# Softmax division moved from the weights to the weighted sum in ten head pairs of a fused mixer

## The chip, the cores and the metric

One Trainium2 chip, one of its cores. The metric is the device time of one execution in microseconds (us). The kernel before took 956.19 us (median of 3 runs, 954.49 to 959.67). Engines are named as in the profile: PE (TensorE, its weight loads PEld), DVE (VectorE), ACT (ScalarE), POOL (GpSimd) and SP, which issues the DMAs.

## The reference

Attention over 4 batches of 12 heads (448 tokens, head size 64), then two mixers (weights `moe_*` and `moe2_*`) on its output of 4 x 448 x 768. All in float32. What the change touches is the attention:

```python
q_n, k_n = (rmsnorm(q, g_q), rmsnorm(k, g_k))
scores = scale * np.matmul(q_n, k_n.transpose(0, 1, 3, 2))
scores = scores - np.max(scores, axis=-1, keepdims=True)
attn = np.exp(scores)
attn = attn / (np.sum(attn, axis=-1, keepdims=True) + 1e-09)
return np.matmul(attn, v).astype(np.float32)
```

The first mixer is relu, a split into two halves, a normalisation, a product over the tokens, a gate and an output product. The second mixes tokens (448 to 256 to 448), then channels (768 to 1536 to 768).

## The kernel before

The 48 heads run as 24 pairs of two heads (`NP`, line 809), six pairs (`KD`) to a batch. A pair goes through these steps, each on four chunks (`C`) of 112 query rows (`T`):

- `norms` and `scale` (lines 622 to 639): row norms of q and k, and the product with them, the latter one POOL operation of 112x1024 in place on `raw`.
- `transposed` (641): q and k turned by PE into a PSUM tile `tp`, copied out by ACT. For the first eight pairs (`WHOLE`) as one float32 tile `whole`, later as a high and a low part.
- `scores` (667): PE writes the scores of both heads to two `sc` tiles; DVE takes the negated maximum `nm`; ACT writes `e`, the exponential, and its row sums to `sums`.
- `normalise` (694): DVE adds 1e-9 to the sums and takes the reciprocal, then POOL multiplies each 112x448 block of `e` in place, eight blocks to a pair.
- `turned` (705): PE transposes `e` (28 transposes to a pair, four to a `tp` tile); ACT or, for two of seven, DVE copies `tp` to `et`.
- `values` (722): PE multiplies by v into the PSUM tile `av`; ACT copies `av` to the high part of `xp`, DVE subtracts to its low part, POOL copies the last tokens to `xr`.

`slot(s)` (773) lists the steps of one slot: the early steps of pair s, and `normalise` of its second half, `turned` and `values` of pair s-1. Beside them the program lists the preparation of weights (`prepare_v`, `prepare_uo`, `prepare_next`: `word`, `wpart`, `wv`) and the first mixer of a batch (`moe`: `vps`, `ups`, `sps`, `xps`), which needs all six pairs of that batch. Then follow the tokens and the channels of the second mixer (`u_ps`, `h1ps`, `h2ps`, `o_ps`).

None of that is the order on the chip. Every operation goes to `Plan`, which knows a cost and a delay for each (`estimate`, line 214) and what it depends on. `issue` (364) places all operations eight times with these costs (`place`), always by due times found from the end backwards, and emits the order of the shortest planned span. So one changed cost can move any operation of the program. A DMA costs max(475, bytes/260) ns there and is taken to land 2000 ns later (line 244). PSUM banks, eight in all, are given out by the plan as well.

Of the kernel before, what the change touches and what calls it, by code (L numbers as in the profile page):

```python
# [12 lines left out]
F32 = mybir.dt.float32  # L13
F32R = mybir.dt.float32r
U32 = mybir.dt.uint32
AF = mybir.ActivationFunctionType
ALU = mybir.AluOpType
# [4 lines left out]
HI, LO = 0, 1  # L22
# [127 lines left out]
class Plan:  # L150
# [63 lines left out]
    def estimate(self, engine, fn, out, ins, kwargs):  # L214

        shape = max((tuple(x.shape) for x in [out] + ins if isinstance(x, Part)), key=free)
        n = free(shape)
        psum = any(x.tile.psum for x in ins)
        if engine == "tensor":
            if fn == "transpose":  # L220
                return ins[0].shape[0] / 1.2 + 3, 200
            n = free(ins[1].shape)
            if ins[1].dtype == F32R:
                return 0.326 * n if ins[0].shape[0] <= 64 else n / 2.4 + 13, 200
            if ins[0].shape[0] <= 64:
                return 1.04 * n, 200
            return n / 1.2 + 54 if out.shape[0] <= 64 else n / 0.6, 200
        if engine == "scalar":
            extra = any(isinstance(kwargs.get(k), Part) for k in ("bias", "scale"))
            extra += kwargs.get("accum_out") is not None  # L230
            return 0.833 * n + (51 if psum else 94) + 93 * extra, 142
        if engine == "vector":
            if n <= 64:
                return 160, 128
            if fn in ("tensor_scalar", "tensor_copy") and not psum:
                return 0.53 * n + 90, 128
            pointer = fn == "scalar_tensor_tensor" and any(free(x.shape) == 1 for x in ins)
            return 1.042 * n + 70 + 61 * pointer, 175 if free(out.shape) < n else 128
        if engine == "gpsimd":
            if fn == "tensor_scalar":  # L240
                return max(165, 1.3 * n + 35), 75
            pace = 2.0 if any(x.steps and x.steps[-1][0] == "to_broadcast" for x in ins) else 2.4
            return max(165, pace * n + 20), 75
        return max(475, shape[0] * n * 4 / 260), 2000

    def fence(self, pools, act):

# [173 lines left out]
def free(shape):  # L421
    n = 1
    for x in shape[1:]:
        n *= x
    return n
# [11 lines left out]
def attention_moe_mixer(  # L437
# [7 lines left out]
    nc = tc.nc  # L445
    B, H, S, D = q.shape
# [5 lines left out]
    P = 128  # L452
    C = 4
    T = S // C
# [83 lines left out]
    ident = const.tile([P, P], F32)  # L538
    make_identity(nc, ident)
    nc = Plan(nc)  # L540

    def opened(stack, name, **kind):
        return stack.enter_context(tc.tile_pool(name=name, bufs=2, **kind))
# [15 lines left out]
    psum = Banks(opened(ctx, "psum", space=PSUM))  # L559

    def mm_tile(name):
        return psum.tile([P, 512], "mm", name)
# [20 lines left out]
    class Attention:  # L583
# [3 lines left out]
        def __init__(self, stack):  # L587
            self.p = Pool(opened(stack, "attn", side="right"))
            self.raw, self.v32, self.r = {}, {}, {}
            self.qt, self.kt, self.e, self.et, self.av = {}, {}, {}, {}, {}  # L590
            self.sums = {}

        def load(self, i):
            if not 0 <= i < NP:
# [46 lines left out]
        def transposed(self, i, a):  # L641
# [6 lines left out]
            tpf = tp.rearrange("p c t -> p (c t)")  # L648
            if i < WHOLE:
                to = self.qt if a == 0 else self.kt  # L650
# [16 lines left out]
        def scores(self, i, c):  # L667
            if not 0 <= i < NP:
                return
            p = self.p  # L670
            if c % 2 == 0:
                self.sums[i, c] = p.tile([P, 4], F32, tag="sum", bufs=4, name="sums")
            sums, qt, kt = self.sums[i, c - c % 2], self.qt[i], self.kt[i]
            nm = p.tile([P, 2], F32, tag="nm", bufs=4, name="nm")
            e = p.tile([T, 2, S], F32, tag="e", bufs=6, name="e")
            sc = [psum.tile([P, 512], "sc", "sc")[:T, :S] for _ in range(2)]
            cs = slice(c * T, (c + 1) * T)
            with nc.joined_up():
                for n, (x, w) in enumerate(PASSES[:1] if i < WHOLE else PASSES):
                    for r in range(2):  # L680
                        me = slice(r * D, (r + 1) * D)
                        if i < WHOLE:
                            nc.tensor.matmul(sc[r], qt[me, cs], kt[me], start=True, stop=True)
                        else:
                            nc.tensor.matmul(
                                sc[r], qt[me, x, cs], kt[me, w], start=n == 0, stop=n == len(PASSES) - 1)
            for r in range(2):
                nc.vector.reduce_max(nm[:T, r:r + 1], sc[r], axis=AX.X, negate=True)
                at = c % 2 * 2 + r
                nc.scalar.activation(  # L690
                    e[:, r], sc[r], AF.Exp, bias=nm[:T, r:r + 1], scale=1.0, accum_out=sums[:T, at:at + 1])
            self.e[i, c] = e

        def normalise(self, i, c0):
            if not 0 <= i < NP:
                return
            sums = self.sums[i, c0][:T]
            nc.vector.tensor_scalar(sums, sums, 1e-9, None, ALU.add)
            nc.vector.reciprocal(sums, sums)
            for c in range(c0, c0 + 2):  # L700
                for r in range(2):
                    e, at = self.e[i, c][:, r], c % 2 * 2 + r
                    nc.gpsimd.tensor_scalar(e, e, sums[:, at:at + 1], 1.0, ALU.mult, ALU.mult)

        def turned(self, i, n):

            if not 0 <= i < NP:
                return
            r, kc = n % 2, n // 2
            t = kc * P + r * (S + R)  # L710
            tp = psum.tile([P, C, T], "tp", "tp")
            for c in range(C):
                nc.tensor.transpose(
                    tp[:, c, :], self.e[i, c].rearrange("p r k -> p (r k)")[:, t:t + P], ident[:T, :T])
            et = self.et[i, n] = self.p.tile([P, S], F32, tag="et", bufs=7, name="et")
            tpf = tp.rearrange("p c t -> p (c t)")
            if n in ON_DVE:
                nc.vector.tensor_copy(et, tpf)
            else:
                nc.scalar.activation(et, tpf, AF.Copy)  # L720

        def values(self, i, kc):

            if not 0 <= i < NP:
                return
            b, j = divmod(i, KD)
            if kc == 0:
                self.av[i] = mm_tile("av")
            av = self.av[i]
            v32, rest = self.v32[i]  # L730
            with nc.joined_up():
                for r in range(2):
                    lhs = v32[:, r, kc] if kc < C - 1 else rest[:, r]
                    rhs = self.et[i, 2 * kc + r if kc < C - 1 else 2 * kc]
                    nc.tensor.matmul(
                        av[r * D:(r + 1) * D, :S], lhs, rhs, start=kc == 0, stop=kc == C - 1)
            if kc < C - 1:
                return

            at = i % XB  # L740
            on = pairs if any(n % XB == at for n in range((B - 1) * KD, NP)) else self.p
            x = on.tile([P, 2, S], F32R, tag=f"xp{at}", bufs=1, name="xp")
            nc.scalar.activation(x[:, HI], av[:, :S], AF.Copy)
            nc.vector.tensor_tensor(x[:, LO], av[:, :S], x[:, HI].bitcast(F32), op=ALU.subtract)
            xr = on.tile([P, 2, R], F32R, tag=f"xr{at}", bufs=1, name="xr")
            nc.gpsimd.tensor_copy(xr, x[:, :, LAST:].bitcast(F32))
            xs_of.setdefault(b, []).append(x)
            xr_of.setdefault(b, []).append(xr)
            self.v32.pop(i)
# [58 lines left out]

    NP = NH // 2
    VB, XB = 2, 9  # L810
    WHOLE = 8
    ON_DVE = (3, 5)
    SLOT = 10
    PREP0, LAG, SPAN = 1, 0.5, 6
# [405 lines left out]
    n = NP + 1  # L1220
# [4 lines left out]
    at = Attention(early)  # L1225
# [79 lines left out]
```

## Time and profile before

| what | us |
|---|---|
| median of 3 runs | 956.19 |
| the profiled execution's own time | 952.84 |
| span of that execution, first to last instruction | 951.1 |
| PE busy in it | 915.1 |
| DVE busy | 567.9 |
| ACT busy | 452.1 |
| POOL busy | 370.1 |

The span is 1.7 us shorter than the execution's own time, which lies 3.4 us under the median. Busy time is the union of the intervals in which an engine had an instruction; since the ends of matmuls are modelled and they overlap in the pipeline, a busy PE need not be at its peak. The granted clock is TensorE's, as a share of 2.4 GHz; its lower level is 1.2 GHz.

### The profile page before, as it was taken

To read this page: it belongs to the slowest core of one execution; us is meant where nothing else is said; L and a number is where in the kernel's file an instruction comes from. 1 tells how busy PE (TensorE), PEld (TensorE's weight loads), DVE (VectorE), ACT (ScalarE), POOL (GpSimd) and SP (SyncE) were. 2 spreads that over 40 slices of the span, in tenths; PEclk is the share of its full clock that TensorE was granted. 3 is DMA by queue.
4 is the path that set the end of the run, shared out by engine and by line. 5 is a ranking of instruction groups with operands and counts; after the bars stand their busy time and mean duration, and the time that the engine had idled before them with its cause. 6 is when DMAs were issued, how large, how long until landed. Compare 5 with 4: busy or idle time off the path is not lost.

```text
span 951.1 us, 15484 instructions
## 1 busy us (share of the span) xinstructions
PE 915.1 (96%) x5328; PEld 736.9 (77%) x5328; DVE 567.9 (60%) x1254; ACT 452.1 (48%) x1135; POOL 370.1 (39%) x538
## 2 busy tenths in 40 slices
PE   3898999999999999999999999999999999999998
PEld 1344366668767777677889999899898998999898
DVE  4787878775776767764151367534665556555434
ACT  5887877777676777765342345301312213122100
POOL 3767766785666664654124123101201102011100
PEclk9998999999999999999999999999999999999999
DMA  6544465666534565332673475721211212111024
GB/s 153 138 101 134 116 172 149 158 188 184 163 92 107 172 207 179 97 98 99 220 223 129 142 246 181 266 85 34 78 56 36 64 34 83 50 51 50 17 89 144
DMA packets 124654, 118.58 MB, mean 125 GB/s; under 512 B 74784, under 2 KB 108128, under 8 KB 123040
## 3 DMA queue, kind: packets, MB, share of 16 engines
q1 hardware_dynamic: 124576, 117.59, 41.0%
q8 instruction: 42, 0.69, 0.3%
q14 instruction: 36, 0.29, 0.1%
HBM read 89.77 MB, written 27.79 MB: 124 GB/s over the span
## 4 chain that ended last, share of the span: by engine, by line
PE 82%; ACT 5%; DVE 5%; DMA 3%; issue 2%; POOL 2%; SPq 1%; ACTq 0%; POOLq 0%; DVEq 0%
PE o_ps L405 18%; PE h2ps L405 18%; PE tp L405 9%; PE av L405 6%; PE xps L405 6%; PE ups L405 6%; PE sc L405 6%; PE sps L405 4%; PE u_ps L405 3%; PE h1ps L405 3%; PE vps L405 3%; ACT e L405 2%; DVE nm L405 1%; SPq L405 1%; DMA x<-x_d 1%
## 5 line engine op out<-in xcount | busy, mean ns | idle before, releaser
L405 PE MATMUL o_ps<-c,h 128*128 128x384 f32 x1008 | 179.7, 337 | 0.0
L405 PE MATMUL h2ps<-ut,c 128*128 128x512 f32 (+1 forms) x864 | 178.9, 364 | 0.0
L405 PEld LDWEIGHTS o_ps<-c,h 128*128 128x128 f32 x1008 | 175.0, 188 | 2.0 <-DVE acc L405 0.5
L405 PEld LDWEIGHTS h2ps<-ut,c 128*128 128x128 f32 x864 | 148.1, 189 | 24.3
L405 POOL TENSOR_SCALAR e<-e,sums 112x448 f32<-112x448 f32 x192 | 122.8, 656 | 63.0 <-DVE sums L405 35.1
L405 POOL TENSOR_TENSOR c<-word,c 128x384 fp32r<-128x384 f32 x40 | 40.5, 1014 | 265.1 <-ACT c L405 241.7
L405 ACT ACTIVATE e<-sc,nm 112x448 f32<-112x448 f32 x192 | 120.0, 637 | 29.1 <-PE tp L405 15.0
L405 DVE TENSOR_REDUCE nm<-sc 112x1 f32<-112x448 f32 x192 | 110.0, 614 | 22.3 <-PE sc L405 22.0
L405 PEld LDWEIGHTS tp<-ident,e 112*128 112x128 f32 x672 | 75.3, 142 | 47.0 <-POOL e L405 16.6
L405 PE MATMUL tp<-ident,e 112*128 112x112 f32 x672 | 101.9, 267 | 6.4 <-POOL e L405 3.2
L405 DVE TENSOR_TENSOR acc<-o_ps,acc 128x384 f32<-128x384 f32 x140 | 77.2, 555 | 29.6 <-PE o_ps L405 28.9
L405 ACT ACTIVATE h<-h2ps 128x512 fp32r<-128x512 f32 (+1 forms) x48 | 25.8, 538 | 116.5 <-PE h2ps L405 114.9
L405 ACT ACTIVATE c<-word 128x384 fp32r<-128x384 f32 x40 | 21.0, 525 | 123.0 <-DVE word L405 58.2
L405 DVE SCALAR_TENSOR_TENSOR h<-h2ps,h 128x512 fp32r<-128x512 f32 (+1 forms) x48 | 29.9, 624 | 82.3 <-ACT h L405 82.2
L405 ACT ACTIVATE et<-tp 128x448 f32<-128x448 f32 x120 | 63.4, 544 | 20.5 <-PE tp L405 19.9
L405 PE MATMUL ups<-xp,wu 128*128 128x448 f32 x288 | 69.6, 379 | 1.4 <-ACT vr L405 0.7
L405 PE MATMUL av<-et,v 128*64 128x448 f32 x288 | 67.4, 563 | 0.0
L405 PE MATMUL xps<-wo,g 128*128 128x256 f32 x432 | 63.3, 291 | 0.1
L405 PEld LDWEIGHTS xps<-wo,g 128*128 128x128 f32 x432 | 55.1, 190 | 5.0 <-issue 2.3
L405 PEld LDWEIGHTS ups<-xp,wu 128*128 128x128 f32 x288 | 51.7, 189 | 8.6 <-ACT vr L405 1.1
L405 DVE TENSOR_SCALAR word<-word 128x384 f32<-128x384 f32 (+1 forms) x92 | 34.2, 372 | 37.1 <-ACT word L405 35.7
L405 PE MATMUL vps<-wv,xp 128*128 128x512 f32 x216 | 55.1, 402 | 0.0
(105 smaller groups left out, 1414.5 us busy)
## 6 DMA issues: line engine op xcount, KB each, us to landing
raw<-in_moe_w_ch_dram SPq DMA_DIRECT2D x40, 384.0 KB, 3.2
wu<-wu_d SPq DMA_DIRECT2D x16, 768.0 KB, 5.1
wo<-wo_d SPq DMA_DIRECT2D x12, 1024.0 KB, 5.1
raw<-in_q_dram SPq DMA_DIRECT2D x48, 112.0 KB, 3.0
acc<-u_d SPq DMA_DIRECT2D x14, 384.0 KB, 8.2
out_dram<-o SPq DMA_DIRECT2D x28, 192.0 KB, 1.9
v<-in_v_dram SPq DMA_DIRECT2D x48, 96.0 KB, 2.6
x_d<-xo SPq DMA_DIRECT2D x36, 128.0 KB, 2.4
```

The costliest lines, as they stand in the source:

```text
L405: getattr(getattr(self.nc, op.engine), fn)(*args, **kwargs)
```

## The change

For the first ten pairs (`AFTER = 10`) `e` is no longer divided by its sums. `divisors` takes the reciprocals of all eight sums columns of the pair at once on DVE, has POOL spread each of them over 64 columns (`wide`), PE turn that with four transposes into a `tp` tile and ACT copy it to `over`, in which each column of `av` finds its divisor. At the end of `values`, DVE multiplies `av` by `over`, ACT copies the product to the high part of `xp` and POOL, not DVE, subtracts to the low part. The other fourteen pairs go on as before. The sums of a pair lie in one tile of eight columns, not in two of four; in the program both maxima are listed ahead of both exponentials; the ring of `et` has six places, not seven. The planned delay of a DMA is now 2400 ns and 1.2 ns for each 1000 bytes, not 2000 ns.

```diff
-        return max(475, shape[0] * n * 4 / 260), 2000
+        size = shape[0] * n * 4
+        return max(475, size / 260), 2400 + 1.2e-3 * size
...
-            if c % 2 == 0:
-                self.sums[i, c] = p.tile([P, 4], F32, tag="sum", bufs=4, name="sums")
+            if c == 0:
+                self.sums[i] = p.tile([P, 2 * C], F32, tag="sum", bufs=3, name="sums")
...
         def normalise(self, i, c0):
...
+            if i < AFTER:
+                if c0 == 2:
+                    self.divisors(i)
+                return
+            sums = self.sums[i][:T, 2 * c0:2 * c0 + 4]
...
+        def divisors(self, i):
+            p, sums = self.p, self.sums[i][:T]
+            nc.vector.tensor_scalar(sums, sums, 1e-9, None, ALU.add)
+            nc.vector.reciprocal(sums, sums)
+            wide = p.tile([T, 2 * C, D], F32, tag="wide", bufs=1, name="wide")
+            nc.gpsimd.tensor_copy(wide, sums.unsqueeze(2).to_broadcast([T, 2 * C, D]))
+            tp = psum.tile([P, C, T], "tp", "tp")
+            for c in range(C):
+                nc.tensor.transpose(
+                    tp[:, c, :], wide[:, 2 * c:2 * c + 2].rearrange("p r d -> p (r d)"), ident[:T, :T])
+            over = self.over[i] = p.tile([P, S], F32, tag="over", bufs=1, name="over")
+            nc.scalar.activation(over, tp.rearrange("p c t -> p (c t)"), AF.Copy)
...
-            et = self.et[i, n] = self.p.tile([P, S], F32, tag="et", bufs=7, name="et")
+            et = self.et[i, n] = self.p.tile([P, S], F32, tag="et", bufs=6, name="et")
...
-            nc.scalar.activation(x[:, HI], av[:, :S], AF.Copy)
-            nc.vector.tensor_tensor(x[:, LO], av[:, :S], x[:, HI].bitcast(F32), op=ALU.subtract)
+            if i < AFTER:
+                over = self.over.pop(i)
+                nc.vector.tensor_tensor(over, av[:, :S], over, op=ALU.mult)
+                nc.scalar.activation(x[:, HI], over, AF.Copy)
+                nc.gpsimd.tensor_tensor(x[:, LO], over, x[:, HI].bitcast(F32), op=ALU.subtract)
+            else:
...
+    WHOLE, AFTER = 8, 10
```

## Rows read from the trace of the kernel before

**Rows 1.** The page: busy us, share of the span and instructions of each engine.

```profile
PE 915.1 (96%) x5328; PEld 736.9 (77%) x5328; DVE 567.9 (60%) x1254; ACT 452.1 (48%) x1135; POOL 370.1 (39%) x538
```

**Rows 2.** Busy us in four stretches: PE, PEld, DVE, ACT, POOL; granted clock; DMA.

```profile
16.00:120.00 104.00, 90.35 (x477) 41.39 (x478) 84.95 (x185) 87.48 (x239) 76.69 (x122) 0.97 0.48 126
120.00:200.00 80.00, 77.00 (x464) 51.60 (x462) 61.92 (x163) 59.94 (x166) 57.05 (x88) 1.00 0.56 157
200.00:480.00 280.00, 279.07 (x1789) 207.32 (x1788) 174.44 (x415) 184.90 (x496) 157.45 (x245) 1.00 0.52 154
480.00:951.00 471.00, 466.88 (x2598) 435.17 (x2596) 243.22 (x487) 114.35 (x226) 74.76 (x71) 1.00 0.31 101
```

**Rows 3.** The same view, stretches of 8 us.

```profile
72.00:80.00 8.00, 7.12 (x42) 4.54 (x43) 5.61 (x7) 5.22 (x13) 6.05 (x10) 0.80 0.34 90
80.00:88.00 8.00, 6.33 (x24) 1.87 (x24) 6.94 (x20) 7.77 (x23) 4.41 (x8) 0.84 0.42 122
```

**Rows 4.** Waits of PE and PEld from 16 to 120 us: total, times, longest.

```profile
PE sc L405 <- ACT e L405: 3.3, 4, 1.5
PE tp L405 <- POOL e L405: 3.2, 9, 0.7
...
PEld sc L405 <- ACT e L405: 16.1, 22, 2.2
PEld tp L405 <- POOL e L405: 14.0, 23, 1.3
```

**Rows 5.** Timeline of PE: start, duration, instructions merged, idle before and its releaser.

```profile
33.25 0.93 PE L405 MATMUL tp<-ident,e 112*128 112x112 f32 x8
...
43.55 0.31 PE L405 MATMUL tp<-ident,e 112*128 112x112 f32 x1
...
71.41 0.32 PE L405 MATMUL tp<-ident,e 112*128 112x112 f32 x1 [0.30 <-POOL e L405]
...
72.61 1.70 PE L405 MATMUL tp<-ident,e 112*128 112x112 f32 x8
```

**Rows 6.** The chain that ended last, in order of time: start, duration, what.

```profile
68.60 2.77 POOL e L405 x4
```

**Rows 7.** Groups of instructions, 16 to 120 us: busy us, mean ns, idle before.

```profile
L405 POOL TENSOR_SCALAR e<-e,sums 112x448 f32<-112x448 f32 x56 | 36.9, 675 | 7.2 <-DVE sums L405 6.1 <-PE sc L405 0.7 <-DVE wpart L405 0.3
...
L405 ACT ACTIVATE et<-tp 128x448 f32<-128x448 f32 x32 | 16.7, 544 | 1.7 <-PE tp L405 1.7
...
L405 DVE TENSOR_TENSOR xp<-av,xp 128x448 fp32r<-128x448 f32 x6 | 3.7, 612 | 0.0
...
L405 DVE TENSOR_SCALAR sums<-sums 112x4 f32<-112x4 f32 x15 | 3.1, 215 | 4.1 <-ACT e L405 4.1
...
L405 DVE RECIPROCAL sums<-sums 112x4 f32<-112x4 f32 x14 | 2.3, 167 | 0.0
```

**Rows 8.** Groups of instructions, the whole trace.

```profile
L405 POOL TENSOR_TENSOR raw<-raw,ry 112x1024 f32<-112x1024 f32 x24 | 46.1, 1921 | 1.3
...
L405 POOL TENSOR_TENSOR tg<-tg,tv 128x448 f32<-128x448 f32 x16 | 18.3, 1148 | 8.3 <-DVE tv L405 5.3 <-ACT tg L405 2.7
```

**Rows 9.** The tile wpart: ns min/median/max, first and last start; then timelines of DVE and POOL.

```profile
L405 DVE TENSOR_SCALAR wpart<-wpart x88: 231/284/3223, 48.0 to 409.5; 128x256 f32<-128x256 f32 x41, 128x256 uint32<-128x256 uint32 x41, 128x192 f32<-128x192 f32 x2, 128x192 uint32<-128x192 uint32 x2
L405 DVE SCALAR_TENSOR_TENSOR wpart<-raw,wpart x88: 345/416/2368, 61.1 to 415.9; 128x256 uint32<-128x256 uint32 x82, 128x192 uint32<-128x192 uint32 x4, 64x256 uint32<-64x256 uint32 x2
...
75.48 3.22 DVE L405 TENSOR_SCALAR wpart<-wpart 128x256 f32<-128x256 f32 x1
...
75.08 2.25 POOL L405 TENSOR_TENSOR raw<-raw,ry 112x1024 f32<-112x1024 f32 x1
77.29 1.26 POOL L405 TENSOR_TENSOR wv<-word,wv 128x512 fp32r<-128x512 f32 x1
```

**Rows 10.** DMA issues: count, KB each, median us from issue to landing.

```profile
wu<-wu_d SPq DMA_DIRECT2D x16, 768.0 KB, 5.1
...
raw<-in_q_dram SPq DMA_DIRECT2D x48, 112.0 KB, 3.0
```

More of the change, by code (lines that the diff above doesn't have):

```diff
@@ L590, in __init__ @@
             self.qt, self.kt, self.e, self.et, self.av = {}, {}, {}, {}, {}
-            self.sums = {}
+            self.sums, self.over = {}, {}
         def load(self, i):
@@ L670, in scores @@
             p = self.p
-            if c % 2 == 0:
-                self.sums[i, c] = p.tile([P, 4], F32, tag="sum", bufs=4, name="sums")
-            sums, qt, kt = self.sums[i, c - c % 2], self.qt[i], self.kt[i]
+            if c == 0:
+                self.sums[i] = p.tile([P, 2 * C], F32, tag="sum", bufs=3, name="sums")
+            sums, qt, kt = self.sums[i], self.qt[i], self.kt[i]
             nm = p.tile([P, 2], F32, tag="nm", bufs=4, name="nm")
@@ L688, in scores @@
                 nc.vector.reduce_max(nm[:T, r:r + 1], sc[r], axis=AX.X, negate=True)
-                at = c % 2 * 2 + r
+            for r in range(2):
+                at = 2 * c + r
                 nc.scalar.activation(
@@ L696, in normalise @@
                 return
-            sums = self.sums[i, c0][:T]
+            if i < AFTER:
[3 more added lines that the diff above has]
+            sums = self.sums[i][:T, 2 * c0:2 * c0 + 4]
             nc.vector.tensor_scalar(sums, sums, 1e-9, None, ALU.add)
@@ L742, in values @@
             x = on.tile([P, 2, S], F32R, tag=f"xp{at}", bufs=1, name="xp")
-            nc.scalar.activation(x[:, HI], av[:, :S], AF.Copy)
-            nc.vector.tensor_tensor(x[:, LO], av[:, :S], x[:, HI].bitcast(F32), op=ALU.subtract)
+            if i < AFTER:
[4 more added lines that the diff above has]
+            else:
+                nc.scalar.activation(x[:, HI], av[:, :S], AF.Copy)
+                nc.vector.tensor_tensor(x[:, LO], av[:, :S], x[:, HI].bitcast(F32), op=ALU.subtract)
             xr = on.tile([P, 2, R], F32R, tag=f"xr{at}", bufs=1, name="xr")
@@ L810, in attention_moe_mixer @@
     VB, XB = 2, 9
-    WHOLE = 8
+    WHOLE, AFTER = 8, 10
     ON_DVE = (3, 5)
```

## The prediction

> **What bounds the kernel now.** The page's busy line came first: PE is busy 915.1 of 951.1 us, no other engine over 60% [rows 1]. So the time is PE's work and the 36 us in which PE stands still, and the next question is where these lie. The busy time by stretches answers it [rows 2]. From 200 to 480 us PE misses 0.9 us, from 480 us to the end 4.1 us. From 16 to 120 us it misses 13.65 of 104, from 120 to 200 us 3.0 of 80; what is left, some 14 us, lies ahead of the first scores, which the change doesn't reach. The stretch from 16 to 120 us is the one to read: pairs 0 to 6 without a mixer, since the first mixer needs six finished pairs. There no engine is full: PE 90.35, ACT 87.48, DVE 84.95, POOL 76.69 of 104 [rows 2]. Such a stage is bound by hand-overs between four nearly even engines.
>
> The waits of that stretch tell who is late: PE stood for ACT's exponential 3.3 us, for POOL's multiplied `e` 3.2 us in nine waits; its weight loads waited 16.1 and 14.0 us for the same two [rows 4]. The timeline of PE shows how the second looks: eight transposes of `e` at a stretch take 0.93 us, but at two places four of them run singly, each 0.31 or 0.32 us with a gap after it; there are eight such rows, the first and the last are shown [rows 5]. At the second place the chain that ended last runs through four POOL multiplications, 2.77 us [rows 6]. Right after, eight transposes took 1.70 us, not 0.93 [rows 5]: the granted clock is 0.80 in 72 to 80 us [rows 3], so 40% of that stretch was at 1.2 GHz.
>
> **The change part by part.**
>
> **POOL's multiplications go.** 56 of them took 36.9 us from 16 to 120 us [rows 7]; ten pairs have 80, about 54 us. What this is worth is not POOL's time but what PE waited: 3.2 us of idle time [rows 4], and in the eight single transposes 0.32 - 0.93/8 = 0.2 us each, 1.6 us more [rows 5]. So -4.8 us; ends 0 (the next wait, for ACT's `e` or DVE's copy, is as late) and -14.0 (all that PEld waited). After that, what comes last for the transposes is ACT's exponential itself.
>
> **The clock.** The stretch at 1.2 GHz behind the second place costs (1 - 0.80) x 8 = 1.6 us [rows 3]; I take -1.6. The next stretch, 0.84, I leave as it is. Ends 0 and -2.9 (both).
>
> **DVE under POOL.** A `wpart` operation with a median of 0.28 us lasted 3.22 us and ended when two POOL operations, 75.08 to 78.55 us, had ended; another, 0.42 in the median, took 2.37 us [rows 9]. Together 4.9 us over their medians. The blockers there are `raw` and `wv`, which stay; but POOL loses 36.9 us and gains about 15 (below) of 76.69, 28%. I take that share, -1.4; ends 0 and -4.9. The Trainium skill, GPSIMD Engine Reference, Specifications, says that VectorE and GpSimd share their SBUF interface and that they contend when VectorE is in a 2-port mode or has two SBUF inputs. The trace agrees (3.22 us for 0.28); by this rule alone the term is anything from 0 to -4.9, as POOL's remaining work falls, and the sum below -3.6 to -8.5.
>
> **Small DVE operations.** Two of four are gone in a pair, 215 + 167 ns = 0.38 us [rows 7]; six pairs, 2.3 us of DVE in a stage where DVE is one of four. I count a fifth, -0.5; ends 0 and -2.3. The new multiplication of `av` takes the place of the subtraction, both PSUM with SBUF, 612 ns [rows 7]: nothing.
>
> **PE gets 40 transposes.** 0.93/8 = 0.116 us each, 0.47 us a pair [rows 5]. For pairs 6 to 9, where PE is full, 4 x 0.47 = +1.9 us. For pairs 0 to 5, 2.8 us among 13.65 us idle [rows 2]; they are wanted only at the end of `values`, so gaps can take them; I count a quarter, +0.7. Ends +1.9 and +4.7.
>
> **ACT gets ten copies.** The nearest row is `et` from the same PSUM shape, 544 ns [rows 7]. Six in the early stage are 3.3 us of a 104 us stretch with 16.5 us idle [rows 2]. Each stands in ACT's queue ahead of exponentials that PE waits for. A fifth on the path, +0.7; ends 0 and +5.4 (ten, all on the path). The high part of `xp` is copied from SBUF instead of PSUM: taken as equal.
>
> **POOL gets two operations a pair.** `wide` is a copy of 112x512 from a broadcast; the nearest row is the product of 112x1024 with a broadcast, 1921 ns [rows 8], so 0.96 us by half of it, and 1.9 us at most. The subtraction of 128x448 costs 1148 ns [rows 8]. About 2.1 us in place of 5.4. They stand ahead of later `raw` and `wpart` work in POOL's queue, but POOL is the least busy engine there. The end of a pair grows: multiply, copy, subtract on POOL, `xr`, some 1.1 us more than before. Only the sixth pair of a batch holds back a mixer, and PE has other pairs then: 0, up to +1.1.
>
> **The planned landing.** 112 KB cost 0.48 + 2.0 us in the plan and now 3.0, the measured 3.0; 768 KB 5.0 and now 6.4, against a measured 5.1 [rows 10]. No DMA gets faster; the plan asks earlier. SP's queue and all orders shift. After 200 us there is 0.9 + 4.1 us to win and little; 0, ends -1.5 and +3.
>
> **Rings, sums and listing order.** Six places for `et` instead of seven leave 6 x 0.54 us of copies ahead: 0. The rest: 0.
>
> Sum: -4.8 - 1.6 - 1.4 - 0.5 + 2.6 + 0.7 = -5.0 us. Against the profiled execution's own 952.84 us that is 947.8 us, 946.1 of span; it lies 3.35 us under the median of the runs, so for the median I say 956.19 - 5.0 = 951.2 us.
>
> **The rivals.**
>
> **ACT and DVE fill the gap (no change).** With POOL away the transposes wait for `e` itself, and PE's waits for ACT (3.3 us, and 16.1 of PEld) take over. Then only the single transposes and half of the idle time go, -3.2, and -0.5, against +2.6 and +0.7: -0.4, 955.8 us. For it: ACT is as full as PE there (87.48 and 90.35). Against: PEld waited nearly as long for POOL as for ACT [rows 4].
>
> **ACT becomes the bound (slower).** One mechanism: ten copies of `over` and the new waits in ACT's in-order queue, each in front of exponentials that free score banks. Price 10 x 0.544 = 5.4 us and PE's whole 4.7, less the 3.2 us of idle that goes: +6.9, 963 us. It decides once PE's waits for ACT from 16 to 120 us grow by more than POOL's go, from 3.3 to beyond 9 us. Against it: 16.5 us of ACT idle in that stretch.
>
> **PE was not near its limit (a larger gain).** From 16 to 120 us PEld is busy 41.39 of 104 us, against 435.17 of 471 after 480 us [rows 2]; if PE's busy 90 us are mostly hand-overs in disguise, the stage can shrink until ACT is full: 87.5 + 3.3 = 90.8, to some 94 of 104. That is -10, +1.9 for pairs 6 to 9: -8.1, 948.1 us, and with the clock's 2.9 us 945. The Trainium skill, Perfetto Trace Analysis, Identifying the Most-Contended Engine, holds that busy matmul time is no measure of headroom and that the share of LDWEIGHTS is a better one. By that rule this stage has the room; the trace shows the share (40%) but not that other engines would let it be used.
>
> **The change doesn't do what it says.** POOL's work goes where PE was full anyway, and the new order of all operations, set by changed DMA delays, loses after 200 us what the early pairs win: +3 - 5 = -2, 954 us. PE's 0.9 us idle from 200 to 480 us says that the plan has plenty to fill with.
>
> **How the numbers follow.** Forecast 0.46 (own range 948 to 955); filled gap 0.22; ACT bound 0.14; larger gain 0.12; undone by the order 0.06. What can be told from no change here is about 0.5%, 4.8 us, so under 951.4 is faster and over 961.0 slower. Of the forecast's 0.46 about 0.29 lie under that bound; with the larger gain and a little of the rest 0.42. Slower: most of the ACT case and the upper ends, 0.15. The rest, 0.43, is no change. The range of 8 in 10 runs from 944 (the larger gain) to 960 (the filled gap with its ends, and part of the ACT case).
>
> **What would show it.** Right: no `e` of POOL among PE's waits before 160 us, no single transposes with gaps, PE's idle time from 16 us to the first `vps` under 9 us, the granted clock above 0.95 in all of it, the first mixer's first `vps` some 5 us earlier. ACT's waits there would tell the filled gap, their growth past 9 us the slower case. PE's total busy time should rise by 2 to 5 us less what the clock gives back. Wrong, if after 200 us PE stands still for more than 6 us, or if the first stretch ends as late as before.

## The result and the profile after

The changed kernel took 948.38 us (median of 4 runs, 946.97 to 950.10) beside 957.45 us (954.49 to 959.67) of the kernel before in the same comparison. The ratio is 0.9913, 95% interval 0.9883 to 0.9942: 9 us, 0.9%, faster. The forecast was 951.2 us in a range of 944 to 960.

The page of the changed kernel, its busy line; the profiled execution took 946.97 us:

```profile
span 944.7 us, 15517 instructions
...
PE 912.2 (97%) x5368; PEld 738.3 (78%) x5368; DVE 574.9 (61%) x1234; ACT 454.1 (48%) x1145; POOL 342.9 (36%) x478
```

Beside [rows 1]: the span is 6.4 us shorter; the two profiled executions lie 5.9 us apart, the medians 9.1, so the traces show about two thirds of the gain. PE's idle time fell from 36.0 to 32.5 us, and its busy time by 2.9 us although it does 40 transposes more. POOL does 60 instructions less. Where the idle time went is in the busy time by stretches (PE, PEld, DVE, ACT, POOL, granted clock, DMA), the changed kernel again:

```profile
16.00:120.00 104.00, 91.64 (x533) 46.05 (x534) 89.21 (x195) 94.06 (x261) 59.75 (x86) 1.00 0.58 159
120.00:200.00 80.00, 79.03 (x475) 54.38 (x475) 65.59 (x156) 62.61 (x173) 49.71 (x70) 1.00 0.54 152
200.00:480.00 280.00, 278.99 (x1784) 206.27 (x1783) 177.24 (x411) 181.13 (x486) 155.18 (x241) 1.00 0.51 149
480.00:944.70 464.70, 460.76 (x2572) 430.20 (x2570) 239.60 (x468) 111.03 (x219) 74.11 (x69) 1.00 0.30 99
```

Against [rows 2], the first stretch holds 533 matmuls, not 477, in the same 104 us; 28 of them are transposes of `wide`, so 28 more come from work that had lain behind. ACT went from 87.48 to 94.06 us, DVE from 84.95 to 89.21; POOL fell by 17 us. PE's idle time is 12.36 us there, not 13.65, and 0.97 us, not 3.0, in the next stretch. The granted clock is 1.00, not 0.97. From 200 to 480 us nothing changed but a few instructions; the last stretch is 6.3 us shorter and holds 26 matmuls fewer, since that much of its work now lies earlier. The first mixer's first `vps` starts at 116.7 us, not 122.1: 5.4 of the 6.4 us are won ahead of it.

The waits of PE from 16 to 120 us in the changed kernel (total, times, longest), to be laid beside [rows 4]:

```profile
PE sc L406 <- ACT whole L406: 6.9, 2, 4.0
PE sc L406 <- ACT e L406: 4.0, 6, 1.1
PE tp L406 <- ACT et L406: 1.3, 4, 0.5
PE tp L406 <- ACT e L406: 1.3, 2, 0.9
```

No wait for POOL's `e` is left. But another grew: two waits for the turned q and k of the first pairs (`whole`) take 6.9 us. The same two in PE's timeline, the kernel before first:

```profile
16.46 4.71 PE L405 MATMUL sc<-whole 64*112 64x448 f32 x12 [1.81 <-ACT whole L405]
...
24.73 1.01 PE L405 MATMUL sc<-whole 64*112 64x448 f32 x4 [1.38 <-ACT whole L405]
```

```profile
16.59 5.00 PE L406 MATMUL sc<-whole 64*112 64x448 f32 x12 [3.97 <-ACT whole L406]
...
26.58 1.76 PE L406 MATMUL sc<-whole 64*112 64x448 f32 x8 [2.94 <-ACT whole L406]
```

The first of them costs nothing here: it lies almost wholly ahead of 16 us, and the first scores start when they did, at 16.59 and 16.46 us. The second is the one that grew within the stretch, by 1.6 us. All waits for ACT together went from 8.9 to 14.7 us, of which 1.4 and 3.4 lie ahead of 16 us.

The singles of [rows 5] are gone too. In PE's timeline of the changed kernel at the same place the transposes come in fours, `wide` among them, and eight take 0.93 us, at full clock:

```profile
67.19 0.60 PE L406 MATMUL tp<-ident,wide 112*128 112x112 f32 x4
67.74 0.60 PE L406 MATMUL tp<-ident,e 112*128 112x112 f32 x4
...
72.39 0.93 PE L406 MATMUL tp<-ident,e 112*128 112x112 f32 x8
```

### The profile page after: what moved, and what is told of

Its sections match the earlier page's. It is cut to its first block, busy times and chain, and to the rows that moved or that the text cites. A ratio compares the mean times of both kernels' runs of the same rounds, so it can differ in the third digit from the quotient of the medians.

```text
span 944.7 us, 15517 instructions
## 1 busy us (share of the span) xinstructions
PE 912.2 (97%) x5368; PEld 738.3 (78%) x5368; DVE 574.9 (61%) x1234; ACT 454.1 (48%) x1145; POOL 342.9 (36%) x478
## 4 chain that ended last, share of the span: by engine, by line
PE 81%; ACT 8%; DMA 4%; DVE 2%; SPq 1%; issue 1%; POOL 1%; ACTq 0%; POOLq 0%
PE o_ps L406 19%; PE h2ps L406 18%; PE tp L406 8%; PE av L406 6%; PE xps L406 6%; PE vps L406 5%; PE sc L406 5%; PE ups L406 5%; PE sps L406 4%; ACT e L406 3%; PE u_ps L406 3%; PE h1ps L406 3%; SPq L406 1%; ACT et L406 1%; DMA x_d<-xo 1%
## 5 line engine op out<-in xcount | busy, mean ns | idle before, releaser
L406 PE MATMUL tp<-ident,e 112*128 112x112 f32 x672 | 96.7, 263 | 3.7 <-ACT et L406 1.3
L406 POOL TENSOR_SCALAR e<-e,sums 112x448 f32<-112x448 f32 x112 | 71.2, 652 | 35.8 <-DVE sums L406 9.0
```

What stands on the lines that cost most here:

```text
L406: getattr(getattr(self.nc, op.engine), fn)(*args, **kwargs)
```

## The experiments

The numbers of a run stand beside the kernel before in the same comparison: 957.13 us for the first four, 957.84 for the next four, 957.64 for the last four.

### Which half of the change: landing times or pairs

The two halves alone. First the new planned landing in the kernel before:

```diff
-        return max(475, shape[0] * n * 4 / 260), 2000
+        size = shape[0] * n * 4
+        return max(475, size / 260), 2400 + 1.2e-3 * size
```

> The kernel before with the new planned landing of a DMA alone; nothing is computed in another way. If the gain comes from POOL's multiplications leaving the way to the transposes (theory POOL), this is within 3 us of the kernel before (954 to 960 us), and PE still waits about 3 us for POOL's e from 16 to 120 us. If it comes from the new order that the landing times give (theory ORDER), this is 947 to 951 us, with PE's idle time from 16 to 120 us down to 12 us or less without any divisor.

Measured: 959.02 us, ratio 1.0023 (1.0011 to 1.0036). Then the ten pairs alone, with the line above taken back in the changed kernel:

> The changed kernel with the old planned landing (2000 ns): the ten pairs alone. Theory POOL: 946 to 951 us, no wait of PE for POOL's e before 160 us, first vps at 115 to 118 us. Theory ORDER: 953 to 958 us, first vps at 121 us or later.

Measured: 957.81 us, ratio 1.0008 (0.9990 to 1.0026). So neither half is worth anything alone, and both together give 9 us: 957.1, 959.0, 957.8, 948.4. Both theories had expected one of the two to carry the gain; both fell. ("The ten pairs" means here all of the change but the planned landing: the smaller ring of `et`, the one tile of sums and the listing order come with them. No run has these without the new division, so what they do to the order is not told apart.) The ten pairs alone do remove POOL from PE's waits, and yet PE stands still. The changed kernel with the old landing, waits of PE from 16 to 120 us and the stretches:

```profile
PE sc L405 <- ACT whole L405: 6.9, 2, 4.2
PE sc L405 <- ACT e L405: 4.3, 5, 2.5
PE tp L405 <- POOL wide L405: 2.1, 2, 1.9
...
16.00:120.00 104.00, 87.63 (x512) 42.35 (x512) 87.65 (x191) 92.42 (x255) 58.75 (x83) 1.00 0.57 158
...
200.00:480.00 280.00, 276.87 (x1770) 203.38 (x1769) 165.61 (x399) 180.68 (x487) 157.11 (x237) 1.00 0.49 148
```

PE misses 16.4 us in the first stretch and 3.1 us from 200 to 480 us, against 12.4 and 1.0 in the changed kernel, with the same operations. (The profiled execution of this kernel took 953.54 us, 4.3 under its median; that of the changed kernel lies 1.4 under its own.)

### What POOL's leaving is worth in a fixed order

The kernel before keeps its order; the 80 multiplications are planned but not issued:

```diff
                     nc.gpsimd.tensor_scalar(e, e, sums[:, at:at + 1], 1.0, ALU.mult, ALU.mult)
+                    if i < LEFT_OUT:
+                        nc.ops[-1].instead = ()
```

> The kernel before, in its own order of all operations, without POOL's multiplications of e in the first ten pairs: the division is left out for these and nothing stands in for it. It is the whole gain that POOL's leaving can bring in a fixed order. Theory POOL: the terms -4.8 (PE's waits and the single transposes), -1.6 (clock) and -1.4 (DVE under POOL) make -7.8, so 949 to 951 us against 957; the stretch at 1.2 GHz around 72 us is gone. Theory ORDER: no more than -2 us, since the next engine in that order is as late.

Measured: 956.20 us, ratio 0.9989 (0.9973 to 1.0005). The prediction's first three terms, -7.8 us together, came out as -0.9, which is not clear of nothing. The busy time of this kernel, first stretch:

```profile
16.00:120.00 104.00, 86.22 (x476) 40.09 (x477) 83.11 (x187) 87.41 (x240) 41.41 (x66) 0.98 0.48 128
```

POOL lost 35 us of work [rows 2]. The matmuls in the stretch are the same number, 476 beside 477; PE did them in 4.1 us less busy time, 3.3 us of it in the transposes of `e` (25.7 us, not 29.0), and stood still 4.1 us longer, 17.8 us. The first `vps` starts at 122.2 us (122.1 before). So what was saved turned into waiting: the other queues keep the order that the plan had made for a POOL at work. The place of [rows 6] shows one such case. In the kernel before, DVE and PE there:

```profile
71.11 0.62 DVE L405 TENSOR_TENSOR xp<-av,xp 128x448 fp32r<-128x448 f32 x1
...
66.22 1.01 PE L405 MATMUL sc<-whole 64*112 64x448 f32 x4
...
71.83 0.98 PE L405 MATMUL tp<-ident,raw 112*128 112x112 f32 x4
```

And without the multiplications:

```profile
70.44 1.68 DVE L407 TENSOR_REDUCE nm<-sc 112x1 f32<-112x448 f32 x3
72.03 0.61 DVE L407 TENSOR_TENSOR xp<-av,xp 128x448 fp32r<-128x448 f32 x1
...
67.13 1.01 PE L407 MATMUL sc<-whole 64*112 64x448 f32 x4
...
69.35 0.79 PE L407 MATMUL tp<-ident,e 112*128 112x112 f32 x6
72.86 0.68 PE L407 MATMUL tp<-ident,raw 112*128 112x112 f32 x4 [2.71 <-DMA wu_d<-wpart]
73.33 1.70 PE L407 MATMUL tp<-ident,e 112*128 112x112 f32 x8
```

Without POOL's 2.77 us PE had done its transposes of `e` by 70.14, not 71.73 us. But the next four, of `raw`, start only at 72.86 us. In both kernels they start 0.1 to 0.2 us after DVE's subtraction from `av` has ended (71.73 and 72.64); it is the last reader of `av`, and the plan gives these transposes the PSUM bank that `av` leaves. It stands in DVE's queue behind three maxima, where the plan had put it while POOL was at work. I read the 2.71 us as that wait; the DMA that the row names is the last event by the profile and writes nothing that PE reads. (In the kernel before, PE's own last single ended at 71.73 us as well, so there the two can't be told apart.) From the scores ahead of this place (66.22 and 67.13 us) to these transposes it takes 5.6 us with the multiplications and 5.7 without, and behind it eight transposes take 1.70 us, as in [rows 5].

### The same the other way round

The changed kernel keeps its order; behind each exponential of the ten pairs POOL multiplies the block by 1.0:

```diff
                 nc.scalar.activation(
                     e[:, r], sc[r], AF.Exp, bias=nm[:T, r:r + 1], scale=1.0, accum_out=sums[:T, at:at + 1])
+                if i < AFTER:
+                    nc.ops[-1].then = e[:, r]
...
+                if x.then is not None:
+                    e = x.then.real()
+                    self.nc.gpsimd.tensor_scalar(e, e, 1.0, 1.0, ALU.mult, ALU.mult)
```

> The changed kernel in its own order of all operations, with a POOL multiplication of every 112x448 block of e of the ten pairs put back behind its exponential (by 1.0, so the result stays): 80 of some 0.64 us. If POOL's absence is needed for the gain, in this order as well as in one of its own: +5 us or more, 953 to 960 us, with PE waiting 3 us or more for POOL's e. If the order alone makes the gain and POOL has room: under +2 us, 948 to 950 us.

Measured: 969.75 us, ratio 1.0128 (1.0086 to 1.0170), 21 us over the changed kernel. So this order has no room for POOL's work at the places where it was put back. But PE did not wait for `e`, as had been expected; it waited for what stood behind the multiplications in POOL's queue. The longest wait, 5.5 us for ACT's `whole`, is of that kind too: ACT stood 3.3 us for a small POOL operation (`ra`) that started behind four multiplications, 25.17 to 28.77 us. Waits of PE from 16 to 120 us, and the stretch:

```profile
PE sc L406 <- ACT whole L406: 9.0, 2, 5.5
PE tp L406 <- POOL wide L406: 6.1, 4, 2.8
...
16.00:120.00 104.00, 79.89 (x438) 40.03 (x439) 84.38 (x156) 79.98 (x218) 80.49 (x122) 0.93 0.49 136
```

The two runs together: taking 80 operations from an order made for them wins 0.9 us; putting 80 into an order made without them loses 21. They are not mirror images, since the operations put back have no planned place; that is also why the 21 us are no price of the multiplications.

### A lucky order, or a gain that stays

If one changed constant moves the kernel by several us, the 9 us may be chance. So the changed kernel with two neighbouring landings:

```diff
-        return max(475, size / 260), 2400 + 1.2e-3 * size
+        return max(475, size / 260), 2300 + 1.2e-3 * size
```

> The changed kernel with 2300 instead of 2400 ns in the planned landing: the same operations, another order. The runs so far: before 957.1, new landing alone 959.0, ten pairs alone 957.8, both 948.4 us. Theory TOGETHER (the divisors win once the plan knows about when data land): 946 to 951 us, first vps at 115 to 118 us. Theory LOTTERY (each plan falls somewhere in a range of ten microseconds, and the changed kernel drew a good one): anywhere from 946 to 960, with a first vps that moves by several us with it.

> The changed kernel with 2500 instead of 2400 ns in the planned landing. TOGETHER: 946 to 951 us and a first vps at 115 to 118 us, as with 2300 and 2400. LOTTERY: it differs from the changed kernel or from the run with 2300 by more than 4 us, in either direction.

Measured: 950.05 us with 2300, ratio 0.9924 (0.9900 to 0.9949), and 948.10 us with 2500, ratio 0.9902 (0.9868 to 0.9935). Both times are what TOGETHER expected. The mark that I had set beside them, a first `vps` at 115 to 118 us, was missed: it starts at 122.6 and 120.6 us, about as late as in the kernel before with 2000 ns (122.1). Against the kernel before at the same landing it looks otherwise, as the table below shows.

The kernel before with another constant in its own form:

```diff
-        return max(475, shape[0] * n * 4 / 260), 2000
+        return max(475, shape[0] * n * 4 / 260), 1900
```

> The kernel before with 1900 instead of 2000 ns in the planned landing: how far the kernel before moves when only its order is drawn anew. LOTTERY: it moves by 3 us or more, and may come near the changed kernel (950 us). TOGETHER: within 3 us of 957, since nothing else changes.

Measured: 967.74 us, ratio 1.0103 (1.0068 to 1.0139): 10 us from 100 ns in the plan. On how far an order moves the time LOTTERY was right and TOGETHER wrong, so one order of each kernel proves little. Then the kernel before with the new form and the two neighbouring values:

> The kernel before with the new form of the planned landing, 2300 ns and 1.2 ns for 1000 bytes; the partner of the changed kernel with 2300 (950.05 us). If the ten pairs bring some 8 to 10 us at like landing, and the kernel before at 2000 ns is one of its better orders: 956 to 968 us. If the kernel before gains from this landing as the changed one does: 948 to 953 us.

> As the run before, with 2500 ns; the partner of the changed kernel with 2500 (948.1 us). Ten pairs worth 8 to 10 us: 956 to 968 us. Landing worth it alone: 948 to 953 us.

Measured: 960.93 us, ratio 1.0044 (1.0028 to 1.0059), and 961.80 us, ratio 1.0052 (1.0035 to 1.0069). In one table, medians in us, and the start of the first `vps` in the profiled execution, without and with the ten pairs:

| planned landing | kernel before | with the ten pairs | difference | first `vps` |
|---|---|---|---|---|
| 1900 | 967.74 | | | 130.7 |
| 2000 | 957.13 | 957.81 | +0.7 | 122.1, 120.4 |
| 2300 + 1.2 per 1000 bytes | 960.93 | 950.05 | -10.9 | 134.3, 122.6 |
| 2400 + 1.2 per 1000 bytes | 959.02 | 948.38 | -10.6 | 130.0, 116.7 |
| 2500 + 1.2 per 1000 bytes | 961.80 | 948.10 | -13.7 | 128.9, 120.6 |

With the new form the ten pairs bring 11 to 14 us in all three orders that were run. The kernel before at 2000 is the best of its five, so the change was compared with a favourable order, which hid some 2 to 5 us. Four orders with the pairs are few, and one of the four shows no gain; that the gain holds with three values of the new form is shown, that it holds in most orders is not.

Where it is won can be read from the last column. At the same landing the ten pairs start the first mixer 8 to 13 us earlier in the three orders that gain, and 1.7 us earlier in the one that doesn't. From the first `vps` to the end all fourteen kernels that were traced take 825 to 835 us, while the first `vps` itself lies between 116.6 and 137.0 us. So most of what an order or the pairs win or lose is decided ahead of the first mixer.

What the pairs take away in those orders is on PE's list of waits, 16 to 120 us; the kernel before with 2300, then with 2500:

```profile
PE tp L406 <- POOL e L406: 6.4, 6, 4.6
PE sc L406 <- ACT e L406: 3.9, 4, 1.9
...
16.00:120.00 104.00, 84.13 (x423) 40.84 (x424) 76.81 (x167) 78.55 (x214) 71.73 (x112) 0.89 0.47 127
```

```profile
PE tp L406 <- POOL e L406: 9.7, 11, 2.9
PE sc L406 <- ACT whole L406: 4.5, 2, 4.2
...
16.00:120.00 104.00, 88.65 (x451) 41.28 (x453) 78.90 (x175) 82.87 (x226) 73.80 (x117) 0.92 0.49 130
```

POOL's `e` costs PE 6.4 and 9.7 us of idle time there, and the clock is at 0.89 and 0.92; with the ten pairs at the same landings it is 0.99 and 0.95. With 2400 the kernel before has 3.8 us of such waits and 0.93. These waits aren't the gain one for one: with the ten pairs PE's idle time in the stretch falls by 3.5 us (2300), 4.3 (2400) and 2.8 (2500), so with 2300 and 2500 other waits took their place in part.

### The price of what was added, and the number of pairs

The changed kernel keeps its order, and what spreads the divisors is not issued (`wide`, its 40 transposes, the copies to `over`; the multiplication becomes a copy):

```diff
             for op in nc.ops[first:]:
+                op.instead = ()
...
                 nc.vector.tensor_tensor(over, av[:, :S], over, op=ALU.mult)
+                nc.ops[-1].instead = "tensor_scalar", (over, av[:, :S], 1.0, None, ALU.mult), {}
```

> The changed kernel in its own order, without what spreads the divisors: no wide on POOL, no 40 transposes of it, no copies to over; the multiplication of av by over is a copy with factor 1.0, so the division is left out for ten pairs. It prices what was added. By the terms of the prediction (PE +2.6, ACT +0.7): 3.3 us under the changed kernel, 945 us. If the early stage hides the added work altogether: 1.9 us under it (the transposes of pairs 6 to 9 alone), 946.5. If ACT's copies are all on the path: 8 to 10 us under it, 939.

Measured: 944.92 us, ratio to the kernel before 0.9874 (0.9855 to 0.9892): 3.5 us under the changed kernel, against 3.3 expected. The four executions of either kernel spread over 3 to 4 us, so this doesn't tell 3.3 from the 1.9 that was expected if the early stage hides the work; it does rule out the 8 to 10. The order was the one made with this work in it, so a new order might win more.

Six pairs, and all 24:

> The changed kernel with six pairs instead of ten. By the prediction pairs 6 to 9 fall where PE is full and cost 4 x 0.47 = 1.9 us of transposes for nothing: 946 to 947 us, faster than the changed kernel. If taking POOL's multiplications away is worth something there too (PE's idle time from 120 to 200 us fell from 3.0 to 0.97 us), or if the new order is worse: 949 to 953 us.

> The changed kernel with all 24 pairs. Where PE is full each pair costs 0.47 us of PE for its four transposes: 14 x 0.47 = +6.6, 955 us. If POOL's leaving is worth as much there as in the early stage: 945 to 948 us.

Measured: 951.70 us, ratio 0.9945 (0.9924 to 0.9967), and 951.77 us, ratio 0.9946 (0.9931 to 0.9961). Six pairs are 3.3 us slower than ten, not 2 us faster; all of them cost 3.4 us, not 6.6. Each of the two is one order; orders of the changed kernel differ by 2 us with the new landing form, those of the kernel before by 10. So neither run prices the pairs beyond the sixth. The trace with six pairs has its loss ahead of the first `vps` (122.6 us, not 116.7; clock 0.95 from 16 to 120 us), and from 120 to 200 us, where most of pairs 6 to 9 fall, PE stands still for 0.7 us, no more than with ten pairs (0.97). No version that computes the result beats the changed kernel clearly; with 2500 ns it is the same.

## Why the prediction was right, and where it was not

The forecast, faster by 5 us, had the right sign and 951.2 us lies close to 948.4; its stage and the waits that go were right. How a wait that goes becomes time was not: its three terms for POOL's leaving were read from the old order and came out near nothing in that order, and the gain came with the new order, which the forecast had put at 0. That the number lies so near is in part luck.

- **What bounds the kernel.** Right: all of the change lies before 200 us, and the idle time that PE lost lies there (1.3 and 2.0 us of 3.5). That no engine is full there was borne out by ACT and DVE, which took 6.6 and 4.3 us more into the first stretch. 5.4 of the 6.4 us of span are won ahead of the first `vps`.
- **POOL's multiplications, -4.8 us.** The waits went, as said. That they would turn into time by themselves is the step that failed: in the kernel's own order it was -0.9 us for this, the clock and DVE under POOL together, where the prediction had -7.8. The end 0 that I gave for it was near the value for a fixed order; at the place that was followed the next wait was for DVE's subtraction from `av`, not for ACT's `e` or DVE's copy. The gain came only where all orders were made anew; which engine's order matters was not separated.
- **The clock, -1.6.** In the profiled executions 0.97 became 1.00 from 16 to 120 us; 3% of 104 us is 3.1 us, the far end of that term. In the fixed order the half clock at that place stayed (0.79 from 72 to 80 us), as did the gap ahead of it; the next stretch went from 0.84 to 1.00. The ten pairs at the neighbouring landings have 0.99 and 0.95, so this part comes and goes with the order. Over all executions the mean clock is 0.993 in the kernel before (29 executions) and 0.997 in the changed one (4). Among those 29 a mean clock lower by 0.001 goes with 0.9 us; by this, as an estimate, the clock makes 3 to 4 of the 9 us, and the term was about half of what came.
- **DVE under POOL, -1.4.** Not there in the changed kernel. The longest `wpart` operations are shorter (1.88 and 2.06 us, not 3.22 and 2.37), but there are more of middling length: the three 128x256 groups on DVE took, over the whole trace, 37.1 + 18.4 + 12.3 = 67.8 us before and 41.7 + 14.1 + 15.0 = 70.8 after. POOL's `raw` stayed, and `xp` came; which of its operations hold DVE was not followed. In the fixed order without POOL's `e` the 3.22 us stayed (3.23), the 2.37 did not come again, and the groups took 65.6 us, 2.2 less, which made no time.
- **Small DVE operations, -0.5.** They went as said (one pair of 168 and 196 ns in place of two), but no run tells what that is worth.
- **What is added, +3.3.** 3.5 measured, within a spread that would also allow 2. The shares in it, a quarter of PE's and a fifth of ACT's, were guesses that this doesn't test one by one. The rows behind it: four transposes of `wide` 0.60 us by themselves, where I took 0.47 in a longer run; `wide` 610 ns, where I took 960 from a product of two inputs; the subtraction 1155 ns in the median (1148); `over` 559 ns (544).
- **Pairs 6 to 9, no gain.** Open. PE's idle time from 120 to 200 us fell from 3.0 to 0.97 us, 2 us that the sum didn't have; but it fell to 0.7 with six pairs too, so these pairs aren't what took it away. Six pairs were slower than ten, by what happens ahead of the first mixer in that order.
- **The planned landing, 0 (from -1.5 to +3).** Alone it was +1.9, within those ends; but it was set beside the other terms as if they could be added. With the ten pairs it is -9.4 (957.8 to 948.4), without them +1.9. That the two depend on each other was in no rival.
- **The rivals.** "Undone by the order" was priced at 3 us, and 100 ns in the plan move the kernel before by 10. With the old landing the ten pairs win 1.7 us up to the first `vps` and lose 2.2 behind it, which is of that kind, but without the changed delays. ACT as the bound did not come: PE's waits of scores for ACT's `e` are 4.0 us, not 9. All waits for ACT behind 16 us did grow, from 7.5 to 11.3 us, by more than the 3.2 us of POOL's that went; that was half of this rival's sign, and yet the time fell. The larger gain, 948.1 us, is the nearest of all to the measured 948.4, and came in part: PEld went from 41.4 to 46.1 us in the first stretch [rows 2], ACT to 94. But the way to the first `vps` became 5.4 us shorter, not ten, with ACT busy 92 of its 101 us, and part of the time is the clock's.
- **The marks.** The first `vps` came at 116.7 us, some 5 us earlier as foretold; in the two neighbouring orders it came no earlier than in the kernel before at 2000 ns, but 8 and 12 us earlier than in the kernel before at their own landing. The clock was above 0.95 throughout. PE's idle time up to the first `vps` fell less than foretold (12.4, not under 9), and PE's busy time, which was to rise by 2 to 5 us less what the clock gives back (3.1 us in the first stretch), fell by 2.9.

Open: why the ten pairs win nothing with 2000 ns, though the clock in the profiled execution is 1.00 from 16 to 120 us as well. PE's waits there are spread over `ACT e`, `wide` and ACT's copies, with none that stands out, and it was one order. Whether a landing delay between 2000 and 2300 decides it, or the part that grows with the size, was not run.

## What to carry to other kernels

Taking work off an engine paid here only where the other engines' queues were put in a new order for it, and not in every new order: in the fixed one, every instruction behind the old hand-over kept its old place. Where the order comes from a plan, compare two versions at several settings of the plan before believing a difference of 1%: here one constant moved the same operations by 10 us. The price of added work, read from the rows, came out near here, within the spread; the price of a wait that goes was an upper end, and the next instruction in the queue of whoever waits says what is left of it. Where one stage sets the pace, its end (here the first `vps`) compared at like settings says more than the sum of the waits.

## What the runs showed that was not expected

A POOL copy of 112x512 from a broadcast took 610 ns, 1.2 ns for an element of a row, against 1.9 ns for the two-input product with a broadcast (1912 ns for 112x1024). Four executions of the changed kernel had a mean granted clock of 1.000, 0.998, 0.996 and 0.994 and took 946.97, 948.57, 948.18 and 950.10 us: the share of time at half clock differs between executions of one program, and the fastest and the slowest of them are the ones with the highest and the lowest mean clock.
